# When the first block's MLP weights are split and where their tiles are taken: adaLN attention and MLP block on one core

## The chip, the cores and the metric

One core of a Trainium2 chip runs the whole program. The metric is device microseconds of one execution: the median of three runs was 2412.84 us (2409.73 to 2415.67). PE is TensorE, DVE VectorE, ACT ScalarE, POOL GpSimd, SP SyncE, whose queue issues the DMAs spoken of here.

## The reference

A transformer block with conditioned LayerNorm (adaLN), S = 2048 rows, D = 576, 32 heads of 18, MLP width 4608. `sa`, `ca`, `ga`, `sb`, `cb`, `gb` are six rows of `silu(c) @ w_mod`.

```python
h = _layernorm(x) * (1 + ca) + sa
x = x + ga * _A_ref(h, A_wqkv, A_wo)     # softmax attention, then @ wo
h = _layernorm(x) * (1 + cb) + sb
x = x + gb * _B_ref(h, B_w1, B_w2)       # silu(h @ w1) @ w2
```

## The kernel before

All operands of matmuls are float32 rounded to a format that PE takes in one pass (fp32r), so precision is kept by splitting: an operand `a` is stored as `hi = round(a)` and `lo = a - hi`, and a product is three matmuls (hi by hi, hi by lo, lo by hi). The weights `wo`, `w1`, `w2` have to be split once.

The work runs over four blocks `b` of 512 query rows. Attention goes through all blocks in a fixed rhythm of slots: scores `psa` for the row maximum (`mx` on DVE, L804), scores `psb` again transposed, `exp` on ACT (`pt`, L854), and `psv` = P V (L889). Between the slots PE is filled with the work of the block before: its output projection (`psp`), residual and second LayerNorm, and MLP. That filler is a list of small functions (`fl.add`), each with an estimated PE time; a planner keeps its own clock `plan.t` and chooses when the next one is emitted. PE's order is written out in this way; the other engines' orders are set by a scheduler from what was emitted and its costs.

The MLP has 36 tiles of hidden units, taken in nine chunks of four (`CH` = 4). For a chunk, `mlp1` makes pairs of tiles with `w1` (`ps<-hh,w1t`), ACT and DVE form SiLU in `etmp`, ACT writes its hi part `g`, POOL its lo part `g` (L1125), and `mlp2` multiplies the four with `w2` (`ps<-w2t,g`) for the four row tiles `j`, in parts 0 to 31. Before it come the projection (`proj`, four `j` of 14 parts), the LayerNorm of each `j` (POOL `x` L1003 adds the second half of the residual, DVE `bn_stats` L1009, POOL `r` L388 the inverse root, DVE L394 to L402, POOL `ob` L403), and the transposes `h_T` (`hh` and `hl` are the hi and lo parts, on POOL L413 and L415). The lo part of the attention output, `tl` (L977), is made on POOL, too.

In block 0 the weights come raw from DRAM, in halves. `weights()` puts an ask in a list; `load_half` (L679, SP) loads a half into one of three `raw` buffers; `split_half` (L692 to L696, POOL) multiplies w2 and wo by their gate (L692), casts to the hi part (L693, or L695 for w1) and subtracts for the lo part (L696); `store_one` (L703, SP) writes the split tile to DRAM scratch, from which blocks 1 to 3 load it (L666). `serve()` runs once in each step of the main loop: it does a store that is due `STORE` ns after its split, splits a half `LAND` ns after its load, and loads a half when fewer than three are in flight. `settle()` forces splits that are still missing when `proj`, `mlp1` or `mlp2` begin. All of these times are the planner's, not the chip's. `w_load` and `w2_load` take the tile from its ring (4 buffers for w1, 5 for w2; `wo` uses the same rings) at the moment they ask, and an ask for w1 passes asks for w2 that have not begun.

Of the kernel before, what the change touches and what calls it, by code (L numbers as in the profile page):

```python
# [10 lines left out]
F32R = mybir.dt.float32r  # L11
# [47 lines left out]
LP = 8000  # L59
PB = 9  # L60
PVMAX, PVMIN = 5, 3
EACH, LAND, STORE = (1500, 2000), 5000, 4000
QKB = 3
GS = 2
GR = [[range(i, min(i + GS, n)) for i in range(0, n, GS)] for n in (28, 27)]
# [26 lines left out]
def f(ap):  # L92
    return ap.bitcast(F32)
# [247 lines left out]
def tile_adaln_block(ctx: ExitStack, tc: tile.TileContext, x, wqkv, wo, w1, w2, c, wfirst, wcol, out):  # L341
# [316 lines left out]
                        fill.add(200, lambda a=mt_: mod_piece(*a), mode="full")  # L658

    asks, flight, stores = [], [], []  # L660
    last_load = [0]

    def weights(key, w, src, scr, first, gate=None):

        if not first:
            nc.sync.dma_start(f(w), f(scr))  # L666
            return
        ask = {"key": key, "w": w, "src": src, "scr": scr, "gate": gate, "n": w.shape[2] // 2, "at": 0, "halves": [0, 1]}
        i = len(asks)
        while key[0] == "w1" and i and asks[i - 1]["key"][0] == "w2" and len(asks[i - 1]["halves"]) == 2:  # L670
            i -= 1
        asks.insert(i, ask)
# [12 lines left out]
    def split_half():  # L685

        _, ask, h, raw = flight.pop(0)
        w, gate, n = ask["w"], ask["gate"], ask["n"]
        cs = slice(h * n, h * n + n)
        hi = w[:, 1, cs]  # L690
        if gate is not None:
            after_pe(nc.gpsimd.tensor_tensor(raw, raw, gate[:, cs], op=ALU.mult))  # L692
            nc.gpsimd.tensor_copy(hi, raw)  # L693
        else:
            after_pe(nc.gpsimd.tensor_copy(hi, raw))  # L695
        nc.gpsimd.tensor_tensor(w[:, 0, cs], raw, f(hi), op=ALU.subtract)  # L696
        if h:
            stores.append((plan.t + STORE, w, ask["scr"]))

    def store_one():  # L700

        _, w, scr = stores.pop(0)
        nc.sync.dma_start(f(scr), f(w))  # L703

    def serve():

        if stores and stores[0][0] <= plan.t:
            store_one()
        if flight and flight[0][0] + LAND <= plan.t:
            split_half()  # L710
        if asks and len(flight) < 3 and last_load[0] + EACH[asks[0]["gate"] is not None] <= plan.t:
            load_half()
# [226 lines left out]
    def prefetch(b):  # L939
        pool = mp["p"]  # L940
        c = ready[b] = {}
        for kt in range(KT):
            if kt < 4:
                w = pool.tile([P, 2, KT * P], F32R, tag="w1", name="wo1", bufs=W1B)[:, :, :D]
            else:
                w = pool.tile([P, 2, D], F32R, tag="w2", name="wo2", bufs=5)
            weights(("wo", kt), w, wo[:, kt, :], wos[kt], b == 0, ga)
            c["wo", kt] = w
        c["x1"] = []
        for j in range(NST):  # L950
            c["x1"].append(pool.tile([P, D], F32, name="x1", bufs=5))
            nc.sync.dma_start(c["x1"][j], x[b * QB + j * P:b * QB + (j + 1) * P, :])

    def post(b):
# [26 lines left out]
        def proj(j, part):  # L981
            if part == 0:
                def ops(g, i):
                    kt, a, w = PASS[i]
                    return (c["tl"] if a else c["th"])[:, kt, j * P:(j + 1) * P], c["wo", kt][:, 1 - w, g * HH:(g + 1) * HH]

                settle(*[("wo", kt) for kt in range(KT)])
                c["pp"] = Pair([bank("psp", psA)[:, :HH] for _ in range(2)], ops, 14, not state["tail"])
            for s in GP[part]:
                c["pp"].step(s)  # L990
            if part == len(GP) - 1:
                for g in range(2):
                    add_x1(j, g, c["pp"].ps[g])
                    plan.op("AV"[g == 0], plan.t + 200, 440, c["pp"].release[g])
# [34 lines left out]
        def h_T(kt):  # L1029
            if kt == 0:  # L1030
                c["hh"] = pool.tile([P, KT, QB], F32R, tag="th", name="hh")
                c["hl"] = pool.tile([P, 4, QB], F32R, tag="tl", name="hl")
            ps = bank("psT", psF)
            chain([("A", 780), ("V", 430)], plan.t, plan.take("f"))
            for j in range(NST):
                nc.tensor.transpose(ps[:, j * P:(j + 1) * P], c["ob"][:, j, kt * P:(kt + 1) * P], ident)
            tmp, hi = etmp(), c["hh"][:, kt, :]
            mod_out(ps, kt, 1, tmp)
            mod_hi(hi, tmp)
            if kt == 4 and not last:  # L1040
                c["h2"] = const.tile([P, D], F32R, tag="ga", name="h2")[:, :QB]
                nc.gpsimd.tensor_copy(c["h2"], tmp)
            mod_lo(kt, hi, c["hl"][:, kt, :] if kt < 4 else None, tmp, nc.vector if last and kt % 2 == 0 else nc.gpsimd)
# [14 lines left out]
        for j in range(NST):  # L1058
            rest(REST[j])
            steps_ = dict(zip((1, 4, 8, 11), ln_steps(j - 1))) if j else {}  # L1060
            for part in range(len(GP)):
                fl.add(MMH * len(GP[part]), lambda j=j, part=part: proj(j, part), need={0: pair_need if j else o_need, len(GP) // 2: half_need}.get(part))
                if part in steps_:
                    fl.add(0, steps_[part])
        for step in ln_steps(3):
# [6 lines left out]
            fl.add(LP)  # L1072

        def w_load(i):
            c["w1", i] = pool.tile([P, 2, KT * P], F32R, tag="w1", name="w1t", bufs=W1B)
            weights(("w1", i), c["w1", i], w1[i], w1s[i], b == 0)

        def w2_load(i):
            c["w2", i] = pool.tile([P, 2, D], F32R, tag="w2", name="w2t", bufs=5)
            weights(("w2", i), c["w2", i], w2[i], w2s[i], b == 0, gb)  # L1080

        def etmp():
            if last:
# [44 lines left out]
        def mlp2(i0, j, part):  # L1128
            if part == 0:
                def ops(g, n):  # L1130
                    a, w = ((0, 0), (0, 1), (1, 0))[n % 3]
                    return c["g", i0 + n // 3][:, a, j * P:(j + 1) * P], c["w2", i0 + n // 3][:, 1 - w, g * HH:(g + 1) * HH]

                settle(*[("w2", i0 + n) for n in range(CH)])
                c["p2"] = Pair([bank("ps2", psF)[:, :HH] for _ in range(2)], ops, 3 * CH, not state["tail"])
            for s in G2[part]:
                c["p2"].step(s)
            if part < len(G2) - 1:
                return
            for hf in range(2):  # L1140
                add_x1(j, hf, c["p2"].ps[hf])
                plan.op("AV"[hf == 0], plan.t + 200, 440, c["p2"].release[hf])
            if i0 + CH == NFT:
                nc.sync.dma_start(out[b * QB + j * P:b * QB + (j + 1) * P, :], c["x1"][j])
# [5 lines left out]
        if not EARLY:  # L1150
            for kt in range(KT):
                fl.add(440, lambda kt=kt: h_T(kt), name=["h_T"], need=hT_need, mode="full")
        for i in range(4):
            fl.add(0, lambda i=i: w_load(i))
        fl.add(0, lambda: w2_load(0))
        if b == 0:
            for i in range(1, 4):
                fl.add(0, lambda i=i: w2_load(i))
        if EARLY:
            if b == 0:  # L1160
                fl.add(LP)
            for kt in range(KT):
                fl.add(440, lambda kt=kt: h_T(kt), name=["h_T"], need=hT_need, mode="full")

        def w_at(n, *loads):

# [4 lines left out]
        def add_mlp1(i, *loads):  # L1171

            for part in range(NG):
                fl.add(MMC * len(GR[not last][part]), lambda part=part: mlp1(i, part), need={0: pair_need, NG // 2: half_need}.get(part))
                w_at(part, *loads)

        def add_mlp2(i0, add, *loads):
            for j in range(NST):
                for part in range(len(G2)):
                    add(MMH * len(G2[part]), lambda j=j, part=part: mlp2(i0, j, part), None, {0: pair_need, len(G2) // 2: half_need}.get(part))  # L1180
                    w_at(j * len(G2) + part, *loads)

        add_mlp1(0)
        for i0 in range(0, NFT, CH):
            if i0 + CH < NFT:
                w2s_ = [(0, w2_load, i0 + 1), (4, w2_load, i0 + 2), (9, w2_load, i0 + 3)] if i0 or b else []
                if i0 == 0:
                    w2s_ += [(1, w_load, 4), (3, w_load, 5)]
                add_mlp1(i0 + 2, *w2s_)
                add_mlp1(i0 + CH, (6, w_load, i0 + 6), (11, w_load, i0 + 7))  # L1190
                add_mlp2(i0, fl.add, (2, w_load, i0 + 8), (9, w_load, i0 + 9), (18, w2_load, i0 + 4))
            else:
                add_mlp1(i0 + 2, (0, w2_load, i0 + 1), (2, w2_load, i0 + 2), (4, w2_load, i0 + 3))
        if last:
            add_mlp2(NFT - CH, fl.add)
        else:
# [481 lines left out]
```

## Time and profile before

| | |
|---|---|
| median of the runs | 2412.84 us |
| the profiled execution | 2407.57 us, its span 2405.8 us |
| mean granted clock of PE | 0.992 |
| largest groups | L804 `mx` on DVE 1319.0 us, L854 `pt` on ACT 1131.5, L852 `psb` on PE 750.1 |
| block 0's weights split, out-projection to last chunk | about 565 to 1115 us |

In the middle of block 0, seven chunks follow one another, and each `mlp2` wants its four w2 tiles. From the timelines of POOL and PE, the last lo part of a chunk's w2 ended, and PE began the chunk's first row tile (24 matmuls, the 22nd being the first that takes that lo part):

| last w2 lo part ended | first w2 matmul | the 22nd, waited or not |
|---|---|---|
| 736.84 | 736.53 | about 737.9, no wait |
| 789.16 | 787.83 | about 789.3, no wait |
| 841.02 | 840.39 | about 841.8, no wait |
| 894.59 | 895.01 | about 896.3, no wait |
| 950.19 | 947.30 | 950.24, waited 0.48 |
| 1002.70 | 1000.08 | 1002.75, waited 0.48 |
| 1057.67 | 1055.66 | 1057.72, waited 0.44 |

The times marked "about" are worked out from the group of 24 matmuls (1.76 us in the first row, evenly spaced). A row of a wait reads: who waited, for whom, us in total, times, longest. In a timeline row the bracket is the idle time of the engine before the instruction, and what ended it.

### The profile page before, as it was taken

How to read it: one execution, taken by the hardware profiler on the slowest of the kernel's cores; microseconds unless marked ns; L12 is line 12 of the kernel's file. 1: busy time of each engine (PE TensorE's matmuls, PEld its weight loads, DVE VectorE, ACT ScalarE, POOL GpSimd, SP SyncE). 2: the span in 40 equal slices, each digit the busy share in tenths (PEclk: the TensorE clock that was granted, in tenths of full speed). 3: DMA queues.
4: the chain of work that ended last, by engine and by line, in shares of the span. 5: the costliest groups of instructions: out<-in, count | busy, mean ns of one | idle time of the engine just before them, and what ended most of it. 6: DMA issues, size and time to landing. Idle time of an engine off the chain costs nothing.

```text
span 2405.8 us, 52151 instructions
## 1 busy us (share of the span) xinstructions
PE 2323.4 (97%) x19844; PEld 1596.2 (66%) x19844; DVE 1775.2 (74%) x3109; ACT 1482.1 (62%) x2734; POOL 637.5 (26%) x769
## 2 busy tenths in 40 slices
PE   6999999998999999998999999999999999989999
PEld 4874444434567766775676777766677777678998
DVE  8768989887878888886887888887877787144333
ACT  5247777775667776675776777775676677722121
POOL 5201011104746676663311111122211111110000
PEclk9999999999999999999999999999999999999999
DMA  7555556445556666665655445554545554336563
GB/s 254 163 173 173 168 170 182 150 159 157 195 191 206 213 223 208 221 220 180 216 172 175 164 164 191 170 181 139 188 160 167 189 166 163 120 113 225 203 206 118
DMA packets 201474, 433.02 MB, mean 180 GB/s; under 512 B 31362, under 2 KB 67618, under 8 KB 201226
## 3 DMA queue, kind: packets, MB, share of 16 engines
q1 hardware_dynamic: 201226, 429.68, 54.5%
q8 instruction: 159, 2.61, 0.5%
q14 instruction: 89, 0.73, 0.1%
HBM read 338.54 MB, written 86.33 MB: 177 GB/s over the span
## 4 chain that ended last, share of the span: by engine, by line
PE 84%; DVE 7%; DMA 4%; ACT 3%; POOL 2%; issue 1%; SPq 0%; ACTq 0%; POOLq 0%; DVEq 0%
PE ps L486 25%; PE psv L889 18%; PE psa L802 13%; PE ps L480 10%; PE psb L852 8%; PE psqk L591 3%; DVE mx L804 3%; PE psp L486 2%; PE psv L486 2%; DMA raw<-in_w 1%; ACT pt L854 1%; PE psqk L486 1%; PE psv L1350 1%; PE psqk L1350 1%; PE psp L480 1%
## 5 line engine op out<-in xcount | busy, mean ns | idle before, releaser
L804 DVE TENSOR_REDUCE mx<-psa 128x1 f32<-128x512 f32 x2048 | 1319.0, 683 | 310.9 <-PE psb L852 161.8
L854 ACT ACTIVATE pt<-psb 128x512 f32<-128x512 f32 x2048 | 1131.5, 598 | 503.1 <-PE psb L852 305.8
L852 PE MATMUL psb<-qt,kb 56*128 56x512 f32 x2048 | 750.1, 423 | 10.7 <-ACT pt L854 9.7
L802 PE MATMUL psa<-ka,qt 54*128 54x512 f32 x2016 | 698.2, 415 | 9.5 <-DVE mx L804 8.0
L802 PEld LDWEIGHTS psa<-ka,qt 54*128 54x128 f32 x2016 | 335.2, 186 | 298.7 <-DVE mx L804 202.0
L889 PE MATMUL psv<-pt,vt 128*32 128x512 f32 x4096 | 513.5, 604 | 2.3 <-ACT ov L893 1.7
L486 PE MATMUL ps<-w2t,g 64*128 64x288 f32 x4992 | 410.5, 294 | 7.7 <-POOL w2t L693 3.9
L486 PEld LDWEIGHTS ps<-w2t,g 64*128 64x128 f32 x4992 | 382.7, 186 | 43.0 <-DVE mx L804 10.1
L852 PEld LDWEIGHTS psb<-qt,kb 56*128 56x128 f32 x2048 | 352.4, 185 | 53.6 <-ACT pt L854 38.4
L486 PE MATMUL ps<-hh,w1t 64*128 64x512 f32 x1944 | 371.6, 395 | 6.8 <-POOL w1t L696 3.1
L486 PEld LDWEIGHTS ps<-hh,w1t 64*128 64x128 f32 x1944 | 220.3, 186 | 44.9 <-DVE mx L804 7.5
L889 PEld LDWEIGHTS psv<-pt,vt 128*32 128x32 f32 x4096 | 99.5, 109 | 215.8 <-issue 208.0
L1125 POOL TENSOR_TENSOR g<-etmp,g 128x512 fp32r<-128x512 f32 x108 | 137.8, 1297 | 392.3 <-ACT g L1124 334.6
L1003 POOL TENSOR_TENSOR x<-x,gt 128x288 f32<-128x288 f32 x116 | 93.6, 807 | 416.9 <-ACT gt L1002 416.9
L486 PE MATMUL ps<-hl,w1t 64*128 64x512 f32 x864 | 198.0, 393 | 0.5 <-POOL hl L413 0.5
L999 DVE TENSOR_TENSOR x<-ps,x 128x288 f32<-128x288 f32 x184 | 83.8, 456 | 124.8 <-PE ps L480 77.1
L480 PE MATMUL ps<-w2t,g 128*128 128x288 f32 x960 | 133.5, 299 | 7.4 <-ACT g L1124 5.9
L480 PEld LDWEIGHTS ps<-w2t,g 128*128 128x128 f32 x960 | 131.1, 191 | 9.9 <-ACT g L1124 6.3
L486 PEld LDWEIGHTS ps<-hl,w1t 64*128 64x128 f32 x864 | 105.3, 186 | 10.8 <-POOL hl L413 0.9
L1121 ACT ACTIVATE eq<-ps 128x512 f32<-128x512 f32 x36 | 21.6, 600 | 146.3 <-PE ps L480 146.3
L480 PE MATMUL ps<-hh,w1t 128*128 128x512 f32 x360 | 106.9, 390 | 0.5 <-DVE hh L415 0.5
L1122 DVE SCALAR_TENSOR_TENSOR etmp<-etmp 128x512 f32<-128x512 f32 x108 | 76.6, 744 | 23.4 <-ACT etmp L1121 23.2
(146 smaller groups left out, 2084.4 us busy)
## 6 DMA issues: line engine op xcount, KB each, us to landing
w1t<-w1s SPq DMA_DIRECT2D x108, 640.0 KB
w2t<-w2s SPq DMA_DIRECT2D x108, 576.0 KB
kb<-kscr SPq DMA_DIRECT2D x512, 108.0 KB
ka<-kscr SPq DMA_DIRECT2D x504, 108.0 KB
w1s<-w1t SPq DMA_DIRECT2D x36, 640.0 KB
w2s<-w2t SPq DMA_DIRECT2D x36, 576.0 KB
vt<-vscr SPq DMA_DIRECT2D x32, 608.0 KB
qt<-qscr SPq DMA_DIRECT2D x128, 108.0 KB
```

Source lines behind the costliest of these rows:

```text
L480: mm(self.ps[late], lhsT=lhsT, rhs=rhs, start=(i == 0), stop=(i == self.n - 1))
L486: done = mm(self.ps[g], lhsT=lhsT[rows], rhs=rhs[rows], start=(s == 0), stop=(s == self.end))
L591: mm(qk_ps[0], lhsT=w[b][:, kt, :], rhs=(hTl if a else hTh)[:, kt, n * 512:(n + 1) * 512], start=(i == 0), stop=(i == 13))
L802: mm(ps, lhsT=t["q"][64 * j:64 * j + 54, hp, stt * P:(stt + 1) * P], rhs=t["a" if ("a", kc, hp) in t else "b", kc, hp][64 * j:64 * j + 54, ...
L804: return lambda: nc.vector.tensor_reduce(t["mx"][:, 2 * j + hp, stt, kc:kc + 1], ps, axis=AX.X, op=ALU.max)
L852: state["pe"] = mm(ps, lhsT=t["b", kt // 4, hp][64 * e:64 * e + 56, kt % 4 * P:(kt % 4 + 1) * P], rhs=t["q"][64 * e:64 * e + 56, hp, :], s ...
L854: nc.scalar.activation(t["P"][kt, hp][:, e, :], ps, AF.Exp, scale=SCALE)
L889: mm(t["ps"][32 * h:32 * h + 32, :], lhsT=t["v"][:, c0:c0 + 32], rhs=t["P"][kt, h // 2][:, h % 2, :], start=(kt == 0), stop=(kt == NKT - 1 ...
L999: nc.vector.tensor_add(c["x1"][j][:, hs], ps, c["x1"][j][:, hs])
L1003: nc.gpsimd.tensor_add(c["x1"][j][:, hs], c["x1"][j][:, hs], t)
L1122: nc.vector.scalar_tensor_tensor(t, t, 1.0, u, op0=ALU.add, op1=ALU.mult)
L1125: (nc.vector if last else nc.gpsimd).tensor_tensor(g[:, 1, :], t, f(g[:, 0, :]), op=ALU.subtract)
```

## The change

- A tile for a split weight is taken when its first half is split (`make()` in `split_half`), no longer when it is asked for. Before that, a store of the tile that had its place in the ring is issued if it is still pending.
- The planner's `LAND` goes from 5000 to 6000 and `STORE` from 4000 to 8000.
- In block 0 the four w2 tiles of the first chunk are asked for in parts 1, 4, 7 and 10 of the first projection `j` = 0; they were asked for behind w1 0 to 3. w1 2 and 3 are asked for behind the fourth and fifth transpose; they were asked for with w1 0 and 1.
- `hold` keeps a w2 split back while its tile lies two or more beyond what `mlp2` has finished with (`c["freed"]`).
- w2 33, 34 and 35 are asked for in parts 22, 23 and 24 of the `mlp2` before the last chunk; they were asked for in the last `mlp1`.

```diff
-EACH, LAND, STORE = (1500, 2000), 5000, 4000
+EACH, LAND, STORE = (1500, 2000), 6000, 8000
...
+    RING = {"w1": W1B, "w2": 5}
...
     def split_half():
 
         _, ask, h, raw = flight.pop(0)
+        if h == 0:
+            tag = ask["key"][0] if ask["key"][0] != "wo" else None
+            while tag and any(it[3] == (tag, ask["key"][1] - RING[tag]) for it in stores):
+                store_one()
+            ask["w"] = ask["make"]()
...
-        if flight and flight[0][0] + LAND <= plan.t:
+        if flight and flight[0][0] + LAND <= plan.t and not (flight[0][1]["hold"] and flight[0][1]["hold"]()):
             split_half()
...
+                if b == 0 and j == 0 and part in (1, 4, 7, 10):
+                    fl.add(0, lambda i=part // 3: w2_load(i))
...
         def w2_load(i):
-            c["w2", i] = pool.tile([P, 2, D], F32R, tag="w2", name="w2t", bufs=5)
-            weights(("w2", i), c["w2", i], w2[i], w2s[i], b == 0, gb)
+            def make():
+                c["w2", i] = pool.tile([P, 2, D], F32R, tag="w2", name="w2t", bufs=5)
+                return c["w2", i]
+
+            weights(("w2", i), make, D, w2[i], w2s[i], b == 0, gb, lambda: i > c["freed"] + 1)
+
+        c["freed"] = CH - 1
...
+            if j == NST - 1:
+                c["freed"] = i0 + 2 * CH - 1
...
-        for i in range(4):
+        for i in range(4 if b else 2):
             fl.add(0, lambda i=i: w_load(i))
-        fl.add(0, lambda: w2_load(0))
-        if b == 0:
-            for i in range(1, 4):
-                fl.add(0, lambda i=i: w2_load(i))
+        if b:
+            fl.add(0, lambda: w2_load(0))
...
+                if b == 0 and kt > 2:
+                    fl.add(0, lambda i=kt - 1: w_load(i))
...
+                final = b == 0 and i0 + 2 * CH == NFT
+                add_mlp2(i0, fl.add, (2, w_load, i0 + 8), (9, w_load, i0 + 9), (18, w2_load, i0 + 4),
+                         *([(22, w2_load, i0 + 5), (23, w2_load, i0 + 6), (24, w2_load, i0 + 7)] if final else []))
             else:
-                add_mlp1(i0 + 2, (0, w2_load, i0 + 1), (2, w2_load, i0 + 2), (4, w2_load, i0 + 3))
+                add_mlp1(i0 + 2, *([(0, w2_load, i0 + 1), (2, w2_load, i0 + 2), (4, w2_load, i0 + 3)] if b else []))
```

PE's order of instructions is the same in both kernels, as is the number of each kind of instruction on every engine. What moves is the order on POOL and SP, and a few places on DVE and ACT.

On POOL between the first projections, before (`x`, `r`, `ob` of the LayerNorm of three row tiles, one after another):

```order
L1003 TENSOR_TENSOR x_6528<-x_6528,gt 128x288
L388 TENSOR_TENSOR r_7192<-ve,mhalf 128x1
L403 COPY ob<-ob 128x64
L1003 TENSOR_TENSOR x_6530<-x_6530,gt 128x288
L388 TENSOR_TENSOR r_7305<-ve,mhalf 128x1
L403 COPY ob<-ob 128x64
L1003 TENSOR_TENSOR x_6532<-x_6532,gt 128x288
```

The same stretch on POOL after the change, from the second row tile's `x` to the third's:

```order
L1011 TENSOR_TENSOR x_6525<-x_6525,gt 128x288
L698 TENSOR_TENSOR raw<-raw,gb 128x288
L699 CAST w2t<-raw 128x288
L388 TENSOR_TENSOR r_7328<-ve,mhalf 128x1
L702 TENSOR_TENSOR w2t<-raw,w2t 128x288
L403 COPY ob<-ob 128x64
L698 TENSOR_TENSOR raw<-raw,gb 128x288 x2
L699 CAST w2t<-raw 128x288 x2
L702 TENSOR_TENSOR w2t<-raw,w2t 128x288 x2
L1011 TENSOR_TENSOR x_6527<-x_6527,gt 128x288
```

One half (gate, CAST, lo part) now surrounds `r`, and two whole halves stand between `ob` and the next `x`.

On POOL at the end of a chunk in the middle of block 0 (the one of 950 us), before: the last two w2 halves, the next w1 half, the `g` pair:

```order
L692 TENSOR_TENSOR raw<-raw,gb 128x288
L693 CAST w2t<-raw 128x288
L696 TENSOR_TENSOR w2t<-raw,w2t 128x288
L692 TENSOR_TENSOR raw<-raw,gb 128x288
L693 CAST w2t<-raw 128x288
L696 TENSOR_TENSOR w2t<-raw,w2t 128x288
L695 CAST w1t<-raw 128x320
L696 TENSOR_TENSOR w1t<-raw,w1t 128x320
L1125 TENSOR_TENSOR g<-etmp,g 128x512 x2
```

And after:

```order
L698 TENSOR_TENSOR raw<-raw,gb 128x288
L699 CAST w2t<-raw 128x288
L702 TENSOR_TENSOR w2t<-raw,w2t 128x288
L698 TENSOR_TENSOR raw<-raw,gb 128x288
L701 CAST w1t<-raw 128x320
L699 CAST w2t<-raw 128x288
L702 TENSOR_TENSOR w1t<-raw,w1t 128x320
L702 TENSOR_TENSOR w2t<-raw,w2t 128x288
L1143 TENSOR_TENSOR g<-etmp,g 128x512 x2
```

The w1 half's CAST and lo part (L701, L702) now stand ahead of the last w2 half's CAST and lo part. It is so in six of the seven chunks (not in the one of 841 us).

On POOL at the first chunk's second pair of `g`, after, where w1 tile 5 is split (before, both lo parts stood ahead of the pair):

```order
L701 CAST w1t<-raw 128x320
L702 TENSOR_TENSOR w1t<-raw,w1t 128x320
L701 CAST w1t<-raw 128x320
L1143 TENSOR_TENSOR g<-etmp,g 128x512 x2
L702 TENSOR_TENSOR w1t<-raw,w1t 128x320
```

The pair of `g` now stands between the last CAST and its lo part.

More of the change, by code (lines that the diff above doesn't have):

```diff
@@ L660, in tile_adaln_block, with weights @@
     asks, flight, stores = [], [], []
+    RING = {"w1": W1B, "w2": 5}
     last_load = [0]
-    def weights(key, w, src, scr, first, gate=None):
+    def weights(key, make, n, src, scr, first, gate=None, hold=None):
         if not first:
-            nc.sync.dma_start(f(w), f(scr))
+            nc.sync.dma_start(f(make()), f(scr))
             return
-        ask = {"key": key, "w": w, "src": src, "scr": scr, "gate": gate, "n": w.shape[2] // 2, "at": 0, "halves": [0, 1]}
+        ask = {"key": key, "make": make, "src": src, "scr": scr, "gate": gate, "n": n // 2, "hold": hold, "halves": [0, 1]}
         i = len(asks)
@@ L697, in split_half @@
         if h:
-            stores.append((plan.t + STORE, w, ask["scr"]))
+            stores.append((plan.t + STORE, w, ask["scr"], ask["key"]))
     def store_one():
-        _, w, scr = stores.pop(0)
+        _, w, scr, _ = stores.pop(0)
         nc.sync.dma_start(f(scr), f(w))
@@ L942, in prefetch, with make @@
         for kt in range(KT):
[L943 to L948, printed above, removed]
+            def make(kt=kt):
+                if kt < 4:
+                    c["wo", kt] = pool.tile([P, 2, KT * P], F32R, tag="w1", name="wo1", bufs=W1B)[:, :, :D]
+                else:
+                    c["wo", kt] = pool.tile([P, 2, D], F32R, tag="w2", name="wo2", bufs=5)
+                return c["wo", kt]
+            weights(("wo", kt), make, D, wo[:, kt, :], wos[kt], b == 0, ga)
         c["x1"] = []
@@ L1074, in w_load, with make @@
         def w_load(i):
-            c["w1", i] = pool.tile([P, 2, KT * P], F32R, tag="w1", name="w1t", bufs=W1B)
-            weights(("w1", i), c["w1", i], w1[i], w1s[i], b == 0)
+            def make():
+                c["w1", i] = pool.tile([P, 2, KT * P], F32R, tag="w1", name="w1t", bufs=W1B)
+                return c["w1", i]
+            weights(("w1", i), make, KT * P, w1[i], w1s[i], b == 0)
         def w2_load(i):
-            c["w2", i] = pool.tile([P, 2, D], F32R, tag="w2", name="w2t", bufs=5)
-            weights(("w2", i), c["w2", i], w2[i], w2s[i], b == 0, gb)
+            def make():
+                c["w2", i] = pool.tile([P, 2, D], F32R, tag="w2", name="w2t", bufs=5)
+                return c["w2", i]
+            weights(("w2", i), make, D, w2[i], w2s[i], b == 0, gb, lambda: i > c["freed"] + 1)
+        c["freed"] = CH - 1
         def etmp():
@@ L1190, in post @@
                 add_mlp1(i0 + CH, (6, w_load, i0 + 6), (11, w_load, i0 + 7))
-                add_mlp2(i0, fl.add, (2, w_load, i0 + 8), (9, w_load, i0 + 9), (18, w2_load, i0 + 4))
+                final = b == 0 and i0 + 2 * CH == NFT
+                add_mlp2(i0, fl.add, (2, w_load, i0 + 8), (9, w_load, i0 + 9), (18, w2_load, i0 + 4),
+                         *([(22, w2_load, i0 + 5), (23, w2_load, i0 + 6), (24, w2_load, i0 + 7)] if final else []))
             else:
-                add_mlp1(i0 + 2, (0, w2_load, i0 + 1), (2, w2_load, i0 + 2), (4, w2_load, i0 + 3))
+                add_mlp1(i0 + 2, *([(0, w2_load, i0 + 1), (2, w2_load, i0 + 2), (4, w2_load, i0 + 3)] if b else []))
         if last:
```

## The prediction

> **What bounds the kernel now.** I read the page first: busy time, then the chain that ended last.
>
> ```profile
> PE 2323.4 (97%) x19844; PEld 1596.2 (66%) x19844; DVE 1775.2 (74%) x3109; ACT 1482.1 (62%) x2734; POOL 637.5 (26%) x769
> ...
> PE 84%; DVE 7%; DMA 4%; ACT 3%; POOL 2%; issue 1%; SPq 0%; ACTq 0%; POOLq 0%; DVEq 0%
> ```
>
> TensorE (PE) is busy 97% of a 2405.8 us span and holds 84% of the chain. The change neither removes nor reorders a matmul, so it can move only PE's idle time and the clock that idle time costs. I therefore asked for PE's waits by their releaser in the stretch where first-block weights are split: 565 to 690 us (projection, LayerNorm, first MLP chunk), 690 to 1080 (the chunks between) and 1080 to 1125 (the last chunk).
>
> ```profile
> PE ps L486 <- POOL w1t L696: 3.1, 1, 3.1
> PE psa L802 <- DVE mx L804: 2.7, 2, 1.8
> PE psb L852 <- ACT pt L854: 2.6, 6, 1.2
> ...
> PE ps L486 <- POOL w1t L695: 1.2, 1, 1.2
> PE ps L486 <- POOL hh L415: 0.8, 1, 0.8
> PE ps L486 <- POOL hl L413: 0.5, 1, 0.5
> ```
>
> ```profile
> PE ps L486 <- POOL w2t L696: 1.4, 3, 0.5
> PE ps L486 <- POOL w2t L693: 0.9, 2, 0.6
> ```
>
> ```profile
> PE ps L486 <- POOL w2t L693: 3.0, 1, 3.0
> PE ps L486 <- POOL w2t L696: 2.3, 2, 2.0
> ```
>
> Columns: total us, times, longest. Waits for split weights come to 4.3, 2.3 and 5.3 us, 11.9 us in all. That is the prize, with some clock on top. In the middle stretch only 2.3 us are lost in seven chunks, because the splits end almost exactly when PE asks: the margin there is nil, which matters below.
>
> **What goes: the first chunk.** POOL at the split of w1 tile 5 (start, duration, instruction, and in brackets the idle time before it with its releaser), the second of ACT's two `g`, then two windows of 2.5 us (columns: PE, PEld, DVE, ACT and POOL busy, then the granted clock):
>
> ```profile
> 665.20 0.46 POOL L695 CAST w1t<-raw 128x320 fp32r<-128x320 f32 x1 [2.37 <-DMA raw<-in_w]
> 665.61 1.69 POOL L696 TENSOR_TENSOR w1t<-raw,w1t 128x320 fp32r<-128x320 f32 x2
> 667.25 2.52 POOL L1125 TENSOR_TENSOR g<-etmp,g 128x512 fp32r<-128x512 f32 x2
> ```
>
> ```profile
> 662.95 0.62 ACT L1124 ACTIVATE g<-etmp 128x512 fp32r<-128x512 f32 x1
> ```
>
> ```profile
> 665.00:667.50 2.50, 0.97 (x4) 0.81 (x6) 0.00 (x0) 0.00 (x0) 2.30 (x4) 0.82 0.65 238
> 667.50:670.00 2.50, 2.50 (x14) 2.00 (x12) 1.19 (x2) 0.70 (x2) 2.27 (x2) 0.50 0.77 311
> ```
>
> PE waited 1.2 us for this tile's hi part and 3.1 for its lo part, then ran at clock 0.50. Afterwards w2's eight halves are gone from here, so w1 4 and 5 load earlier; but in the new POOL order two `g` operations stand between the last CAST and the last lo part. ACT's second `g` is done at 663.57, so POOL's first of the pair runs before that and the second (half of 2.52) until 664.9; the lo part (half of 1.69) then ends near 666 instead of 667.3. The 1.2 us go, 1.3 of the 3.1 go, and 0.7 of the clock: **-3.2 us** (bounds -1.5, if the pair starts later, and -6.1, if nothing is late: 4.3 plus 1.8 for the clock, of which the second window alone lost half of 2.5).
>
> Before that, the transposes of h: w1's splits stood among the `hl` operations.
>
> ```profile
> 632.96 0.44 POOL L695 CAST w1t<-raw 128x320 fp32r<-128x320 f32 x1
> 633.48 1.27 POOL L415 TENSOR_TENSOR hh<-etmp,hh 64x512 fp32r<-64x512 f32 x1
> ```
>
> ```profile
> 635.00:637.50 2.50, 2.50 (x17) 0.87 (x19) 0.69 (x1) 0.60 (x1) 2.50 (x4) 0.67 0.42 123
> 637.50:640.00 2.50, 2.50 (x16) 0.73 (x8) 0.28 (x1) 0.24 (x1) 1.53 (x3) 0.65 0.75 271
> ```
>
> With w1 2 and 3 asked behind h's third and fourth tile, these splits move behind `hh`, which starts earlier by this CAST (0.44) and by the lo parts ahead of it. The waits of 0.8 and 0.5 go, and with PE fed about 1.5 of clock: the two windows lost a third each, 1.7 together. **-2.8 us** (-1.0, if the clock drops all the same, to -3.4). The longest wait for `pt`, 1.2 us, stands behind DVE operations that run beside POOL's gone splits; I take half of it: **-0.6** (0 to -1.2).
>
> **What goes: the last chunk.** POOL did three `tl` operations ahead of a w2 lo part that PE wanted.
>
> ```profile
> 1104.17 3.77 POOL L977 TENSOR_TENSOR tl<-ou,th 128x512 fp32r<-128x512 f32 x3
> ```
>
> ```profile
> 1124.22 0.54 PE L486 MATMUL psp<-wo,th 64*128 64x288 f32 x4
> ```
>
> ```profile
> 1110.00:1112.50 2.50, 0.22 (x2) 0.22 (x2) 0.00 (x0) 0.00 (x0) 2.42 (x4) 0.56 0.72 272
> 1112.50:1115.00 2.50, 2.24 (x14) 1.92 (x16) 0.78 (x2) 0.54 (x2) 0.60 (x1) 0.50 0.43 177
> ```
>
> Asked at parts 22 to 24 of the chunk before, tiles 33 to 35 are split some 10 us earlier, ahead of all `tl`. Both waits go (5.3), and 1.5 of clock: 2.24 us of PE work at 0.50 lost 1.1, and I take 0.4 for what ran on into the next window. What is late next would be `tl`, but the projection that takes it starts at 1124.22, and with w2's splits gone from between them `tl` only comes sooner. **-6.8 us** (-5.3 to -7.2).
>
> Gains: 3.2 + 2.8 + 0.6 + 6.8 = **13.4 us** (7.8 to 17.9).
>
> **What is added: between the projections.** Eight w2 halves move to 588-614 us. The cost of one half, from groups in the middle stretch (ns min/median/max), and the LayerNorm chain it joins, on POOL and on DVE:
>
> ```profile
> L692 POOL TENSOR_TENSOR raw<-raw,gb x58: 795/809/1256, 705.0 to 1079.9; 128x288 f32<-128x288 f32 x58
> L693 POOL CAST w2t<-raw x57: 417/425/932, 705.8 to 1078.0; 128x288 fp32r<-128x288 f32 x57
> L696 POOL TENSOR_TENSOR w2t<-raw,w2t x57: 795/809/1144, 706.3 to 1078.5; 128x288 fp32r<-128x288 f32 x57
> ```
>
> ```profile
> 600.21 0.24 POOL L403 COPY ob<-ob 128x64 f32<-128x64 f32 x1 [1.45 <-DVE ob L402]
> 601.24 0.81 POOL L1003 TENSOR_TENSOR x<-x,gt 128x288 f32<-128x288 f32 x1 [0.79 <-ACT gt L1002]
> ```
>
> ```profile
> 603.31 0.45 DVE L1009 BATCH_NORM_STATS2 st<-x 128x6 f32<-128x288 f32 x1
> ```
>
> A half is 0.81 + 0.43 + 0.81 = 2.05 us. POOL idled most of this stretch, so most of the 16 us is hidden. Not hidden: two halves stand, on POOL, between `ob` and the next `x`. 600.21 + 0.24 + 4.1 = 604.6 is the earliest for `x`, against 601.24; `bn_stats` could then start at 605.4 instead of 603.31, and DVE runs in order, so every `mx` behind it waits, and PE's `psa` behind that. I take 2.4. Three `r` behind a gating operation may each lose up to 0.81; I take 0.7 for all, as two of three halves should be done. DVE's small operations behind `r` run beside a lo part on POOL: if they are blocked, by up to that part's 0.81 a tile, if not, by nothing; no row of before shows the pair, and I take 0.3 a tile, 1.2. **+4.3 us** (+1.0, if DVE's own queue hides the late `x`, to +6.5).
>
> The Trainium skill, "SBUF — State Buffer", section "SBUF: two separate sides", says that a vector operation with two SBUF inputs and a GpSimd operation take one shared port pair in turn, the loser blocked for the whole instruction. By that rule every one of the four tiles pays, and the term is +6.3 instead of +4.3; no run here shows it yet.
>
> **What is added: the middle chunks.** In six of seven, POOL's new order has the next w1 tile's CAST and lo part (0.45 + 0.87) ahead of the last w2 half's lo part. At 950 and 1001 us before:
>
> ```profile
> 949.39 0.80 POOL L696 TENSOR_TENSOR w2t<-raw,w2t 128x288 fp32r<-128x288 f32 x1
> 950.13 0.45 POOL L695 CAST w1t<-raw 128x320 fp32r<-128x320 f32 x1
> 950.66 0.88 POOL L696 TENSOR_TENSOR w1t<-raw,w1t 128x320 fp32r<-128x320 f32 x1
> ...
> 1001.90 0.80 POOL L696 TENSOR_TENSOR w2t<-raw,w2t 128x288 fp32r<-128x288 f32 x1
> 1004.68 0.45 POOL L695 CAST w1t<-raw 128x320 fp32r<-128x320 f32 x1 [1.99 <-PE psa L802]
> ```
>
> ```profile
> 1000.09 2.96 SPq L679 DMA_DIRECT2D raw<-in_w  x3
> ```
>
> ```profile
> 949.37 0.40 PE L486 MATMUL ps<-w2t,g 64*128 64x288 f32 x2 [0.58 <-POOL w2t L693]
> 950.24 0.53 PE L486 MATMUL ps<-w2t,g 64*128 64x288 f32 x3 [0.48 <-POOL w2t L696]
> ```
>
> PE already waited for the lo part that ended at 950.19, so there each microsecond counts. The swap alone costs 0.45 + 0.88 = 1.33 a chunk. Worse, the CAST now holds POOL until its raw half has landed: one issued at 1000.09 was used at 1004.68, a lag of at most 4.6. If it is 4.6, the last lo part ends at 1004.68 + 0.45 + 0.42 + 0.88 + 0.80 = 1007.2, 4.5 late; if the half has landed when POOL gets there, 1.33. By the table of the chunks in the section on the profile, three of the six have no margin, one 0.2 us, and two (738 and 896) 1.0 and 1.8. Swap alone: 3 x 1.33 + 1.1 + 0.3 + 0 = 5.4. Full lags, some 3 us more in four chunks than the swap: 17. I take 2.5 for each of the four and 2 for the pair together, between the two, since the CAST at 950.13 began with no wait and the one at 1004.68 with 2: **+12 us** (+4, if a wait behind it was due anyway, to +17).
>
> **The sum.** -13.4 + 4.3 + 12 = **+2.9 us**. The profiled execution took 2407.57 us, 5.3 below the median of the runs, 2412.84; I carry the difference over: 2410.5 there, **2415.7** for the median.
>
> **Rivals.**
> *Faster.* The raw halves land in time and LayerNorm's slack covers the halves: costs 4 + 1, gains 13.4, sum -8.4: 2404.4. For it: PE's loss is in few, named places, and POOL is 26% busy. Against: the nil margins in the middle stretch.
> *Slower.* The w1 CAST blocks POOL for its landing in every chunk: +17, the LayerNorm term +6.5, and two waits long enough to drop the clock, at 1.5 us each: +26.5 - 13.4 = +13.1: 2425.9. It decides where the raw half lands over 3 us after its place on POOL is reached.
> The clock term has its rows above: PE idle 3.1 us, then 0.82 and 0.50. The Trainium skill, "TensorE: Matmul & The Clock Gate", section "Part 1: The HAM clock gate", puts the drop at an idle window of about 3.4 us; by that rule waits of 2.5 us, as I forecast, leave the clock alone, and the term is nil but in the slower case. The trace agrees for 1 us waits (0.58 and 0.48 at 950).
> *The first-chunk wait stays.* The lo part behind `g` is as late as before, so that this part does not do what it says: 3.2 less gain, +6.1: 2418.9, still within the bound.
>
> **How the numbers follow.** A measurement of this kernel tells 0.3%, 7.2 us, from no change: 2405.6 to 2420.1. Chances: forecast 0.48 (its own range 2407 to 2420), first-chunk wait stays 0.06, faster rival 0.22, slower rival 0.24. Split by sign: the forecast and the stays-case are mostly inside the bound, and the two rivals mostly outside, which gives faster 0.24, same 0.50, slower 0.26. The range takes in both rivals' centres and leaves their far ends: 2402 to 2427.
>
> **What would show it.** After: no PE wait for `w2t` at 1105-1113, and clock 1.0 there (right on the last chunk); no wait for `hh` at 635; a wait of 2 to 3 us for `w1t` L702 near 663; new waits for `mx` at 604-608, of 2 to 4 us; and in the middle stretch waits for `w2t` of 12 us in place of 2.3 plus. If that last sum stays under 5, I have the lag wrong and the time is near 2404; over 17, it is near 2426. If the waits are as forecast and the time isn't, a shift of the attention pipeline took them up, since PE's waits for `mx` and `pt` share the same stretch.

## The result, and the profile after

| kernel | median us (runs) | lowest to highest | ratio to before, 95% interval |
|---|---|---|---|
| before | 2412.84 (17) | 2409.09 to 2417.28 | |
| changed | 2405.93 (17) | 2402.27 to 2413.47 | 0.9976 (0.9966 to 0.9986) |

The change makes the kernel 0.24% faster, 5.8 us by the ratio (3.4 to 8.2) and 6.9 us by the medians. The forecast was 2.9 us slower: its range held the time, its sign was wrong. Two of the timed runs below, one of before (2550.87 us) and one of `b_land6` (10778.56 us), were far slower than the rest and are left out of the ratios.

The profiled execution of the changed kernel does not show that gain. It took 2411.22 us, longer than the profiled execution of before (2407.57). The page, then the view of the core's clock, of the changed kernel:

```profile
PE 2328.7 (97%) x19844; PEld 1598.7 (66%) x19844; DVE 1774.9 (74%) x3109; ACT 1481.1 (61%) x2734; POOL 638.0 (26%) x769
```

```profile
core 0: 2409.1 us, clock 0.989
```

And the clock of the kernel before:

```profile
core 0: 2405.8 us, clock 0.992
```

The clock records of these profiles hold two values only, 1 and 0.5. So a mean clock of 0.989 over 2409 us means that about 53 us ran at half speed (2 x 0.011 x 2409); before, about 38 us. The timed runs go the other way: a mean clock of 0.9899 over 33 runs of before (49 us) and 0.9914 over 29 of the changed kernel (41 us). So the profiled run of before was a lucky one and that of the changed kernel an unlucky one. Waits can be read from the pair, the total cannot.

PE's waits by releaser in the changed kernel, in the same three stretches as before (565:690, 690:1080, 1080:1125):

```profile
PE psa L808 <- DVE mx L810: 6.4, 4, 4.3
PE psp L486 <- POOL tl L985: 1.5, 1, 1.5
PE psb L858 <- ACT pt L860: 1.3, 5, 0.3
PE ps L486 <- POOL w1t L702: 1.3, 1, 1.3
...
```

```profile
PE ps L486 <- POOL w2t L699: 5.3, 3, 2.3
PE ps L486 <- POOL w2t L702: 3.7, 4, 1.2
```

```profile
PE psb L858 <- ACT pt L860: 1.5, 2, 1.2
PE ps L486 <- ACTq L497: 0.7, 1, 0.7
...
```

The waits for w1t fell from 4.3 to 1.3 us, those for `hh` and `hl` went, and no wait for w2t is left in the last chunk (5.3 before). In their place stand 6.4 us for `mx` between the projections (2.7 before) and 9.0 us for w2t in the middle chunks (2.3 before).

One middle chunk of the changed kernel on POOL, and PE's wait behind it:

```profile
1008.54 1.26 POOL L698 TENSOR_TENSOR raw<-raw,gb 128x288 f32<-128x288 f32 x1
1012.04 0.45 POOL L701 CAST w1t<-raw 128x320 fp32r<-128x320 f32 x1 [2.24 <-DMA raw<-in_w]
1012.43 0.43 POOL L699 CAST w2t<-raw 128x288 fp32r<-128x288 f32 x1
1012.82 0.86 POOL L702 TENSOR_TENSOR w1t<-raw,w1t 128x320 fp32r<-128x320 f32 x1
1013.64 0.79 POOL L702 TENSOR_TENSOR w2t<-raw,w2t 128x288 fp32r<-128x288 f32 x1
```

```profile
1012.91 0.40 PE L486 MATMUL ps<-w2t,g 64*128 64x288 f32 x2 [2.33 <-POOL w2t L699]
1014.48 0.84 PE L486 MATMUL ps<-w2t,g 64*128 64x288 f32 x3 [1.17 <-POOL w2t L702]
```

POOL stands idle 2.24 us with a w2 half in hand that is already multiplied by its gate, because the w1 CAST ahead of it waits for its DMA. This is the wait that the prediction described.

### The profile page after: what moved, and what is told of

The parts are those of the page before. It is cut to its first block, busy times and chain, and to the rows that moved or that the text cites. A ratio compares the mean times of both kernels' runs of the same rounds, so it can differ in the third digit from the quotient of the medians.

```text
span 2409.1 us, 52150 instructions
## 1 busy us (share of the span) xinstructions
PE 2328.7 (97%) x19844; PEld 1598.7 (66%) x19844; DVE 1774.9 (74%) x3109; ACT 1481.1 (61%) x2734; POOL 638.0 (26%) x769
## 4 chain that ended last, share of the span: by engine, by line
PE 83%; DVE 6%; DMA 4%; POOL 3%; ACT 3%; issue 2%; SPq 0%; ACTq 0%; POOLq 0%; DVEq 0%
PE ps L486 24%; PE psv L895 17%; PE psa L808 13%; PE ps L480 10%; PE psb L858 8%; PE psqk L591 3%; DVE mx L810 2%; DMA raw<-in_w 2%; PE psv L486 2%; PE psp L486 1%; ACT pt L860 1%; POOL w2t L702 1%; PE psqk L486 1%; PE psv L1372 1%; PE psqk L1372 1%
## 5 line engine op out<-in xcount | busy, mean ns | idle before, releaser
L596 POOL TENSOR_TENSOR qkhl<-qt,qkhl 128x512 fp32r<-128x512 f32 x24 | 30.9, 1288 | 231.3 <-ACT qt L595 135.4
```

## The experiments

Each kernel was timed against the kernel before on the same chip; a ratio is to that. PE runs the same instructions in the same order in all of them, so profiles can be set side by side stretch by stretch: the time from one given matmul to another, less the same in the first profile of before.

| stretch (us of before) | before again | changed | changed again | LAND 5000 | LAND 5000 again |
|---|---|---|---|---|---|
| 0-577, ahead of the projections | -0.1 | +2.4 | +3.7 | +2.3 | +6.9 |
| 577-626, projections and LayerNorm | +1.9 | +5.8 | +4.1 | -0.4 | -0.6 |
| 626-657, transposes, first mlp1 | -1.4 | -4.9 | -4.9 | -4.9 | -4.9 |
| 657-690, w1 4 and 5 | +2.3 | -2.6 | -2.6 | -4.8 | -5.5 |
| 690-1097, middle chunks | -0.2 | +12.3 | +13.6 | +0.1 | -0.7 |
| 1097-1130, last chunk | +0.5 | -6.8 | -5.6 | -5.2 | -6.0 |
| 1130-2406, blocks 1 to 3 | -2.1 | -3.1 | +1.3 | -2.9 | -3.5 |

The first and last rows hold hardly any change in the order, and still differ by up to 4.6 us between two profiles of one kernel: half-speed stretches fall differently there (in the changed kernel PE ran at half speed from about 161 to 167 us, in before not).

**Both kernels once more.**

> The kernel before, once more, for a second profiled execution and for the clock of each run. If the spread of a few us between runs of one kernel is the clock's (stretches of 3.4 us at half speed whose phase falls anew in each run), the waits of PE by releaser stay as they were (3.1 and 1.2 us for w1t near 663, 3.0 and 2.3 for w2t near 1110), the half-clock stretches change, and runs with a lower mean clock are longer by about 0.4 us for each us at half speed. If instead the waits themselves vary, the same waits come out otherwise by more than 1 us. Time against before: 1.000 within 0.15%.

Measured: 2409.68 us, ratio 0.9995 (0.9986 to 1.0004). Some waits came out otherwise by more than 1 us: 2.7 us for w1t L695 (1.2 before), and 0.6 for w2t L696 in the last chunk (2.3 before).

> The changed kernel, once more. Clock theory: the waits for w2t in the middle stretch are again about 9 us and those for mx at 604-616 about 6 us, with other half-clock stretches than the first profile's, in fewer of the middle chunks; span 2401 to 2406 rather than 2409. Rival (waits vary): w2t waits of the middle stretch under 5 us in this execution. Time 0.9976 of before, within 0.1%.

Measured: 2405.86 us, ratio 0.9983 (0.9971 to 0.9994). The waits came back: 8.6 us for w2t in the middle stretch (5.8 and 2.8), 6.4 for `mx`. The expected span did not: this profiled execution had a span of 2415.2 us at a clock of 0.988, the longest of its 12 runs. Over the timed runs, span and mean clock are correlated by -0.6 (before) and -0.7 (changed). So the larger waits go with the order, and the few us between runs of one kernel come in part from the clock: a correlation of -0.6 to -0.7 leaves half of their variance or more to other causes.

**LAND alone.** The changed kernel with before's value, and before with the new one:

```diff
-EACH, LAND, STORE = (1500, 2000), 6000, 8000
+EACH, LAND, STORE = (1500, 2000), 5000, 8000
```

> The change with LAND at 5000 as before, all else as changed. On POOL the middle chunks then stand as in the kernel before (last w2 half ahead of the next w1 half). Order theory (the swap in the middle chunks comes from LAND alone and costs PE some 7 us of waits and more in clock): 7 to 13 us less than the changed kernel, 2393 to 2399, w2t waits of the middle stretch about 2.3 us. Rival (the swap is covered, the profiled waits were that one execution's): within 3 us of the changed kernel, about 2406.

Measured: 2394.31 us, ratio 0.9930 (0.9918 to 0.9942), and the same kernel later 2393.40, 0.9927 (0.9909 to 0.9945). Its waits for w2t in the middle stretch:

```profile
PE ps L486 <- POOL w2t L702: 1.1, 3, 0.5
PE psb L858 <- DMA qt<-mscr: 0.6, 1, 0.6
PE ps L486 <- POOL w2t L699: 0.3, 1, 0.3
```

1.4 us, where the changed kernel has 9.0. This version is faster than both kernels, 0.7% below before.

> The change with LAND at 5000, once more, beside the two others of this call: 2394, ratio 0.993 within 0.1%. No wait for w2t in the last chunk, under 2 us of them in the middle stretch, mx waits between the projections of about 5 us.

The ratio and the w2t waits came as expected; the `mx` waits were 5.0 us.

```diff
-EACH, LAND, STORE = (1500, 2000), 5000, 4000
+EACH, LAND, STORE = (1500, 2000), 6000, 4000
```

> The kernel before with LAND at 6000 and nothing else changed. POOL's middle chunks then stand as in the changed kernel. Order theory: 7 to 14 us more than before, 2420 to 2427, w2t waits of the middle stretch about 9 us. Rival (the swap is covered): within 3 us of before.

Measured: 2424.01 us, ratio 1.0051 (1.0038 to 1.0064): 12.4 us more than before. The w2t waits of the middle stretch are 8.1 us. But the first chunk pays here, too, in a wait that the prediction did not name:

```profile
PE ps L486 <- POOL w1t L695: 9.4, 2, 5.7
```

Its stretch 657-690 is 8.8 us longer than before's, and 690-1097 is 7.6 us longer. So this kernel shows that LAND costs, not how much of it lies in the middle.

**LAND for a part of the tiles.** `LAND` in `serve()` becomes a number by tile; `early6` has 6000 for wo and tiles 0 to 3, `late6` for all others:

```diff
-        if flight and flight[0][0] + LAND <= plan.t and not (flight[0][1]["hold"] and flight[0][1]["hold"]()):
+        if flight and flight[0][0] + (6000 if (flight[0][1]["key"][0] == "wo" or flight[0][1]["key"][1] < 4) else 5000) <= plan.t and not (flight[0][1]["hold"] and flight[0][1]["hold"]()):
```

> The change with LAND at 6000 for wo and the first chunk's tiles alone, 5000 for the rest. POOL then stands between the projections as in the changed kernel (two halves between ob and the third x), and in the middle chunks as before. Order theory: the LayerNorm term by itself, 4.3 us more than with LAND at 5000 throughout, 2397 to 2400, an mx wait of about 4 us near 606. Rival (the term is the same with any LAND): 2394, within 2 us.

Measured: 2394.49 us, ratio 0.9938 (0.9924 to 0.9951): 0.2 to 2.7 us more than LAND 5000 throughout, by medians or ratios, which the intervals don't tell from none. The wait itself is there:

```profile
PE psa L808 <- DVE mx L810: 7.4, 5, 4.3
```

Against 5.0 us with LAND 5000, where one half stands between `ob` and the third `x` instead of two. So the second half costs PE about 2.4 us more in waits, and the time hardly shows it. What the one half costs, this kernel does not tell.

> The change with LAND at 6000 for all tiles but wo and the first chunk's. The middle chunks stand as in the changed kernel, the projections as with LAND at 5000. Order theory: the middle term by itself, 7 to 12 us more than with LAND at 5000 throughout, 2401 to 2406, w2t waits of the middle stretch 8 to 9 us. Rival (what LAND 6000 costs comes from the projections): 2394 to 2396.

Measured: 2406.50 us, ratio 0.9976 (0.9962 to 0.9990): 11 to 12 us more than LAND 5000 by the ratios (0.0046 to 0.0049 of 2412). Its w2t waits in the middle stretch:

```profile
PE ps L486 <- POOL w2t L702: 4.5, 6, 1.2
PE ps L486 <- POOL w2t L699: 4.0, 3, 2.8
```

8.5 us. So the stretch from w1 tile 5 on holds nearly all of what LAND 6000 costs. Not all of it need be the middle chunks': this kernel also has the lo part of w1 tile 5 behind `g` again (1.3 us of waits for w1t L702), and in its profile the stretch 690-1097 is 8.0 us longer than before's, where LAND 5000 has +0.1 and -0.7. Its `mx` waits between the projections are 6.3 us, with POOL's order there as with LAND 5000 (5.0), so these waits vary by more than 1 us in one order.

**The two new places, one taken out at a time**, both with LAND 5000:

```diff
-                final = b == 0 and i0 + 2 * CH == NFT
+                final = False
...
-                add_mlp1(i0 + 2, *([(0, w2_load, i0 + 1), (2, w2_load, i0 + 2), (4, w2_load, i0 + 3)] if b else []))
+                add_mlp1(i0 + 2, (0, w2_load, i0 + 1), (2, w2_load, i0 + 2), (4, w2_load, i0 + 3))
```

> The change with LAND at 5000, and without the early asks for the last chunk (w2 33 to 35 asked as before). By the term of the prediction: 6.8 us more than the change with LAND at 5000 (2394), so 2401. Rival, clock theory (the profiled execution of before had fewer us at half clock than the mean of its timed runs, so its rows show too little for each wait): 8 us or more, 2402 to 2405.

Measured: 2400.60 us, ratio 0.9953 (0.9941 to 0.9965): 5.5 to 6.3 us more by the ratios. That is the prediction's term, not the larger one.

```diff
-                if b == 0 and j == 0 and part in (1, 4, 7, 10):
-                    fl.add(0, lambda i=part // 3: w2_load(i))
...
-        for i in range(4 if b else 2):
+        for i in range(4):
             fl.add(0, lambda i=i: w_load(i))
-        if b:
-            fl.add(0, lambda: w2_load(0))
+        for i in range(1 if b else 4):
+            fl.add(0, lambda i=i: w2_load(i))
...
-                if b == 0 and kt > 2:
-                    fl.add(0, lambda i=kt - 1: w_load(i))
```

> The change with LAND at 5000, and without the new places of the first chunk's asks (w2 0 to 3 and w1 2 and 3 asked as before). By the terms of the prediction the first chunk is worth 6.6 us less what the LayerNorm pays (1 to 6.5): 2395 to 2400. Rival, clock theory: 9 us or more, since the three waits there (3.1, 1.2 or 2.7, 1.3) each may drop the clock: 2403 to 2406. Last chunk: no w2t wait at all.

Measured: 2400.88 us, ratio 0.9958 (0.9943 to 0.9973): 6.6 to 7.5 us more than the two LAND 5000 measurements, between the two expectations. The old waits are back:

```profile
PE ps L486 <- POOL w1t L702: 3.5, 1, 3.5
PE psb L858 <- ACT pt L860: 2.9, 7, 1.2
PE ps L486 <- POOL hl L413: 1.8, 2, 1.4
```

Here the sum did not close: the two places bring some 6 and 7 us, both together with LAND 5000 bring 17. About 4 to 5 us were without an owner. With LAND 5000 and neither place, the only edit left that moves an instruction is STORE.

**STORE alone**, on before, and taken back from the changed kernel with LAND 5000:

```diff
-EACH, LAND, STORE = (1500, 2000), 5000, 4000
+EACH, LAND, STORE = (1500, 2000), 5000, 8000
```

> The kernel before with STORE at 8000 and nothing else changed (with LAND at 5000, and without the new places of the asks, the changed code gives this same order on POOL and SP). Measured so far, in medians: the two new places are worth 6.6 and 6.3 us when taken out one at a time, both together with LAND at 5000 bring 17.5. Store theory: the missing 5 us are STORE's, which the prediction gave no term: 2405 to 2409 here, and the projection's wait for th near 580 (1.8 to 2.4 us) is gone or shorter. Rival (chance in the medians, or the two places help one another): within 2 us of before, 2410 to 2414.

Measured: 2406.40 us, ratio 0.9978 (0.9968 to 0.9988): 5.3 us less than before by the ratio, 5.8 by the medians.

> The change with LAND and STORE both as before (5000, 4000). Store theory: 4 to 6 us more than with STORE at 8000, 2398 to 2401, with a wait for th near 580 again. Rival: 2394 within 2 us.

Measured: 2398.40 us, ratio 0.9944 (0.9924 to 0.9965), against 2393.40 with STORE 8000 timed beside it: 4.1 to 5.0 us more, though the two intervals overlap. Both runs were made with LAND 5000; no run takes STORE back with LAND 6000. Where the 5 us come from can be seen in PE's waits at the start of the projections (574 to 590 us). First before:

```profile
PE psp L486 <- POOL th L971: 1.8, 1, 1.8
PE psp L486 <- POOL tl L977: 1.6, 1, 1.6
PE psp L486 <- POOL th L979: 0.5, 1, 0.5
```

Then before with STORE 8000:

```profile
PE psp L486 <- POOL tl L977: 1.0, 1, 1.0
PE psp L486 <- POOL th L979: 0.8, 1, 0.8
```

The first and longest wait is gone. In before it was for a `th` CAST on POOL that itself waits for the DMA `ou<-ov`:

```profile
579.62 0.61 POOL L971 CAST th<-ou 128x512 fp32r<-128x512 f32 x1 [4.29 <-DMA ou<-ov]
```

On SP's queue these five DMAs, before and then with STORE 8000:

```profile
572.52 4.99 SPq L917 DMA_DIRECT2D ou<-ov  x5
```

```profile
575.02 3.89 SPq L917 DMA_DIRECT2D ou<-ov  x5
```

It is the same in the other profiles: with STORE 4000 (four profiles) the five issues take 4.7 to 5.0 us and the wait for this `th` is 1.8 to 2.4; with STORE 8000 (ten profiles) they take 3.9 to 4.1 us, and in none is that wait over 0.8. After the three waits, before's clock fell (its windows of 2.5 us):

```profile
580.00:582.50 2.50, 0.62 (x6) 0.40 (x6) 0.00 (x0) 0.00 (x0) 2.13 (x4) 0.75 0.62 185
582.50:585.00 2.50, 2.01 (x10) 1.66 (x12) 0.00 (x0) 0.00 (x0) 1.19 (x1) 0.50 0.51 186
585.00:587.50 2.50, 2.50 (x24) 2.50 (x22) 1.29 (x2) 1.08 (x2) 0.00 (x0) 0.50 0.01 3
```

In before with STORE 8000 the same stretch ran at 1.00 throughout. It does not always: in the changed kernel, which has STORE 8000 too, the three waits there came to 3.0 us (0.8, 1.5 and 0.7) and the clock fell to 0.50 between 585 and 590 us. So the shorter wait is seen in every profile with STORE 8000, the saved clock in five of the ten. On the path between lie the places of wo's stores on SP and of wo's gate operations on POOL, the two things that differ there in the order; which of them sets the five DMAs free earlier was not tried apart.

**LAND smaller still** (4000, STORE 8000):

> The change with LAND at 4000. In the middle chunks the last w2 half then stands a step further ahead of the next w1 half, and POOL may stall on raw halves that have not landed. Order theory: the margin at the start of mlp2 grows, the last 1.4 us of w2t waits go, and it is 0 to 3 us less than with LAND at 5000, 2391 to 2394. Rival (landing: a split asked 4 us after its load waits for the half and holds POOL): 2396 to 2402.

Measured: 2401.79 us, ratio 0.9954 (0.9938 to 0.9970): slower than LAND 5000. The rival's range holds the time, but what the profile shows is not its reason. The middle stretch is 1.4 us shorter than before's and w2t waits there are 1.5 us. What costs is a wait of 4.2 us for `mx` between the projections, where POOL waits for no raw half, and one at the start of the last chunk, where ACT, which releases it, had waited 4.78 us for the DMA `ou<-ov`:

```profile
PE ps L486 <- ACTq L497: 4.6, 1, 4.6
```

## Why the prediction was wrong

In us, by the ratios to before:

| part | forecast | measured | from |
|---|---|---|---|
| first chunk, with its cost between the projections | -6.6 + 4.3 = -2.3 | -4.8; with LAND 5000, -6.8 to -7.5 | `early6` less `land5_nofirst`; LAND 5000 less `land5_nofirst` |
| of it, the second half ahead of the third `x` | no term of its own | +1.9 to +2.7 | `early6` less LAND 5000 |
| last chunk | -6.8 | -5.5 to -6.3 | `land5_noend` |
| middle chunks | +12 | +11 to +12, with w1 tile 5's lo part | `late6` |
| STORE | no term | -5.3 | `b_store8` |
| whole change | +2.9 | -5.8; the parts add up to -4.8 - 5.9 + 11.5 - 5.3 = -4.5 | |

Each measured part is uncertain by some 3 us to either side, so the sum of the parts and the whole agree within the noise.

- **The step that failed first is one that is not in the sum.** The prediction went through the three stretches where split weights were late, and gave STORE's new value no term. It moves only a few rows on SP and POOL, some of them ahead of the projections, where PE had three waits in a row (1.8, 1.6 and 0.5 us). They stood in the same table of waits as the rows quoted, and were passed over because their releasers are `th` and `tl`, not weights. That is 5.3 of the 8.7 us between forecast and result, if STORE is worth with LAND 6000 what it was worth with 5000.
- **The second is the first chunk with its cost between the projections**: -4.8 us instead of -2.3. Of the 8.7 us this is 2.5, hardly more than the noise. How it divides between the gain (-6.6) and the LayerNorm term (+4.3) is open, since in every run the w2 halves that leave the first chunk come to stand between the projections. The mechanism of the LayerNorm term was right. `x` was late (607.11 in the profile after 601.24 before, of which PE was 2.9 us behind already), `bn_stats` waited 1.6 us for it, and PE 4.3 us for `mx`:

```profile
607.94 0.46 DVE L1017 BATCH_NORM_STATS2 st<-x 128x6 f32<-128x288 f32 x1 [1.64 <-POOL x L1011]
```

PE's waits for `mx` rose from 2.7 us (1.8 in before again) to 6.4, near what was forecast. The term for the blocked DVE operation was right in kind: in the changed kernel

```profile
593.71 0.76 DVE L394 TENSOR_TENSOR t<-r 128x1 f32<-128x1 f32 x1 [0.67 <-POOL r L388]
594.50 0.16 DVE L395 TENSOR_TENSOR t<-t,ve 128x1 f32<-128x1 f32 x1
```

the first operation behind `r`, which takes 0.16 us in before, takes 0.76 beside the lo part on POOL from 593.64 to 594.45, and it ends as that does. The two tiles after it pay the same (0.76 and 0.74). So a tile pays 0.6 us, where the prediction took 0.3. The Trainium skill ("SBUF — State Buffer", section "SBUF: two separate sides") has the loser blocked for the whole instruction, from which the prediction had worked out 0.8; the trace agrees in that the blocked operation ends with the other one.
- **The gains of the first chunk.** In the profiles the transposes gave 4.9 us (forecast 3.4 with the first mlp1), and w1 4 and 5 gave 2.6 (forecast 3.2) with `g` ahead of the lo part, as predicted, and 4.8 to 5.5 with LAND 5000, where the lo part stands ahead of `g`. One reading behind the 3.2 was wrong: the matmul that had waited 3.1 us began at 666.53, when the first of the two lo parts ended, which stood behind the CAST that waited 2.37 us for its raw half. The prediction priced the second, ending at 667.3.
- **The middle chunks were right in mechanism, and in size by some luck**: +12 forecast, +11 to +12 measured. The forecast was all waits, with no term for the clock. The profile shows w2t waits of 9.0 us where 12 plus 2.3 were expected, so 6.7 more than before, and about as much again in clock: three drops of 3.4, 3.4 and 6.8 us at half speed, where before has none between 690 and 1097 us. The last chunk came out near its forecast.
- **The carry-over to the median was wrong in its reason**, though it did not touch the sign. The 5.3 us between the profiled execution of before and its median were taken as an offset common to both kernels. They are about what the clock of that one execution explains (38 us at half speed against a mean of 49, of which half is lost time), and the changed kernel's execution was off the other way: the profiled pair says +3.6 us, the medians -6.9.

## What to carry to other kernels

A planner's constant is an edit like any other: of each one that changes, ask for the rows that it moves, also far from the stretch that it was meant for, and give each a term. Here one constant (LAND) cost about as much as the two deliberate moves brought, and taking it back alone made the better kernel. When a bottleneck engine pays for waits in clock as well, one profile of each kernel gives the waits but not the total; take the size of an effect of a few us from timed runs of kernels that differ in one part.

## What the runs showed of the hardware

PE's clock falls after waits that are each well under the length of the drop. In the chunk shown above, after waits of 2.33 and 1.17 us (windows of 2.5 us in the changed kernel):

```profile
1010.00:1012.50 2.50, 0.58 (x9) 0.34 (x5) 0.34 (x1) 0.77 (x2) 0.46 (x2) 1.00 0.39 130
1012.50:1015.00 2.50, 0.92 (x6) 0.70 (x8) 0.00 (x0) 0.00 (x0) 2.50 (x4) 0.78 0.08 15
1015.00:1017.50 2.50, 2.50 (x21) 2.50 (x19) 1.35 (x2) 1.08 (x2) 2.42 (x4) 0.50 0.80 280
1017.50:1020.00 2.50, 2.50 (x19) 2.12 (x17) 1.17 (x3) 1.02 (x3) 2.01 (x3) 0.50 0.66 206
1020.00:1022.50 2.50, 2.50 (x22) 1.15 (x22) 1.73 (x3) 1.53 (x3) 2.06 (x3) 0.85 0.96 355
```

The half speed lasted about 6.8 us. In the second profile of the changed kernel the waits at this place were 0.58 and 1.17 us, and the clock fell all the same, for about 3.4 us (0.62 and 0.70 in the windows from 1012.5 to 1017.5). In before they were 0.30 and 0.48, and it stayed at 1.00. So several short waits close together were enough, with PE busy 1.5 of 5 us in the first case, and no single wait was as long as the shortest drop (3.41 us). That speaks against reading the rule of the Trainium skill ("TensorE: Matmul & The Clock Gate", section "Part 1: The HAM clock gate") as a bound on a single wait, as the prediction did when it let waits of 2.5 us off. The section also says that the window runs freely, and the runs bear that out. In all fourteen profiles each stretch at half speed inside the span lasts 3.41 us or a whole multiple of it, and those of one profile start on one grid of 3.41 us: in the changed kernel at 583.84, 611.14, 669.17, 795.47, 959.30 and 1013.92 us, which are 8, 17, 37, 48 and 16 such steps apart. From one execution to the next this grid lies elsewhere.
